# First weight by one casting load, phi transposed on chip, 128-row tiles of q, k and v, and 14 half tiles of output

## The chip, the cores and the metric

One NeuronCore of a Trainium2 chip. The metric is the device time of one execution in microseconds (us); lower is better. The profile's span runs from the first instruction of the program to the last.

## The reference

Two stages. First an attention over batch 4, 8 heads, 768 positions, head dimension 64, with scores `q k^T / 8`. Three of the heads (`is_retrieval`) use a causal mask. The other five keep, within the causal part, only the first 4 positions and a window of the last 64. A softmax over the keys and the product with `v` follow.

```python
scores = np.where(mask[None, :, :, :], scale * np.matmul(q, k.transpose(0, 1, 3, 2)), -1e9)
a = np.exp(scores - np.max(scores, axis=-1, keepdims=True))
a = a / (np.sum(a, axis=-1, keepdims=True) + 1e-09)
attn_out = np.matmul(a, v)
x = attn_out.transpose(0, 2, 1, 3).reshape(3072, 512)
```

Then a soft mixture of experts on the 3072 rows of `x`. `phi` is 512 x 32 (8 experts with 4 slots each), `w1` is 8 x 512 x 1024, `w2` is 8 x 1024 x 512, all float32.

```python
logits = x @ phi
d = softmax(logits, axis=0)              # over the 3072 rows
slot_input = (d.T @ x).reshape(8, 4, 512)
slot_out[e] = np.maximum(slot_input[e] @ w1[e], 0) @ w2[e]
out = softmax(logits, axis=1) @ slot_out.reshape(32, 512)
```

## The kernel before

**Order of the work.** The kernel does not write its instructions down directly. Each piece of work is an operation of a planner (`Plan`): a name, the engines that may run it with a cost for each, a due time (`key`), the operations it depends on, and the buffers it takes (`acq`) and gives back (`rel`). `Plan.run` places the operations one after another by these costs, and the instructions are emitted in that order. The list `SHIFTS` moves the due times of single operations and fixes some of them to ACT or DVE. Buffers come in classes: 11 large slots in SBUF (`S8`), two PSUM banks for transposes (`TR`), two for scores (`SC`), one for attention sums (`PV`), two memories each for transposed q and k (`QT`, `KT`), one for transposed v (`VT`), and so on. Within an engine the order is fixed by the plan.

**Loads.** All large loads go through POOL's DMA queue and cast float32 to bfloat16 on the way, in one order (`dma`, at most eight in flight). First come the halves of batch 0: q, k and v of heads pairs 0 and 1, then of 2 and 3, 768 KB of float32 each. Then w0, then q, k, v of batch 1, two weights, batch 2, three weights, batch 3, and the other weights. A weight has 2 MB of float32. w0 is special: its first quarter comes uncast, 512 KB over SP's queue, into the memory of `expT` (`sp_front`), and two POOL casts (`o_w0`) bring it into place; the other three quarters come by POOL's queue. SP's queue also brings the retrieval flags, once for each of 128 partitions, and phi by two loads whose contiguous pieces are 32 floats. The last five weights go into memory that attention gives back late; w14 and w15 (the last two of `w2`) come as halves of 256 output columns, first both left halves, then both right halves.

**Attention.** q, k and v arrive in rows of 32 positions. For batches 1 to 3 each of the nine (tensor, batch) loads fills 96 partitions of a slot. `transposes` turns it by four groups of 16 TensorE transposes (L577), each group evacuated by one copy of 768 elements per partition on DVE or ACT (L323, L321). There are 16 pairs `p = 4 b + n` of heads (n and n + 4). For a pair: five score products (`QK`, L610) of up to four 128 x 128 blocks for both heads, laid out by `PGROUPS`; an exponential on ACT for each (L679); three mask products on DVE (`MK`, L626), only for blocks on the diagonal and next to it; then `PV` (L740), its normalization (L761), and transposes of the result (`XT`, L773). One of the 21 blocks of a pair doesn't fit into the five groups: it is computed for all four pairs of a batch in a tile of its own (`QX`, exponential at L704). Before, that is block (0, 5): keys 0 to 127 for queries 640 to 767, which needs no mask.

**Experts.** At each batch's end `LG` (logits), `EL` (their exponential), `DS` (slot sums) and `TE`/`EE` (transposed exponentials into `expT`). After the last batch: `SI`, `H` (first layer, L915), `TH`, `W2` (second layer, L953, one step for each expert). In the gaps stand matmuls on zeros (`Z`, L902; `ZF`, L493, and `ZG`, L504, near the start).

**Output.** `RW` (L980) makes the sums of the row softmax by 24 small matmuls on PE, `RWR` (L986) their reciprocals on DVE; `SO` (L992, L994) puts half of the slot outputs into bfloat16. An output tile is one matmul (`OM`, L1009), a scaling by the reciprocal on ACT or DVE (`OE`, L1017, L1019), and a share of a store (`ST`, L1028). The first 12 of the 24 tiles of 128 rows are done in halves: the left 256 columns as soon as the left halves of w14 and w15 are there, stored over POOL's queue, and the right ones after the right halves, over SP's. The other 12 are done and stored whole, over SP's queue.

Of the kernel before, what the change touches and what calls it, by code (L numbers as in the profile page):

```python
# [10 lines left out]
F32 = mybir.dt.float32  # L11
# [5 lines left out]
KB = 512  # L17
# [144 lines left out]
def act(cols, extra=0.0):  # L162
# [4 lines left out]
SHIFTS = [-192, 84, -330, 309, -90, -87, 300, -18, 120, -42, -48, -360, -132, -240, 42, -360, 57, -222, 12,  # L167
# [28 lines left out]

PGROUPS = [
    [(0, 0, 4)],
    [(1, 1, 4)],
    [(2, 2, 4)],  # L200
    [(3, 3, 3), (0, 4, 1)],
    [(4, 4, 2), (5, 5, 1), (1, 5, 1)],
]
MGROUPS = [(0, 1), (2, 3), (4,)]
PCOL, PGRP = {}, {}
for _g, _parts in enumerate(PGROUPS):
    _c = 512 * _g
# [891 lines left out]
```

## Time and profile before

| | |
|---|---|
| median of the runs | 150.85 us (150.83, 150.85, 151.16) |
| the profiled execution | 150.66 us |
| its span | 148.9 us |
| PE, DVE, ACT, POOL busy | 84%, 73%, 73%, 23% of the span |
| read from HBM, written | 52.50 MB, 6.29 MB |
| mean granted TensorE clock | 0.959 |

The page divides the span into 40 slices of 3.7 us and gives for each the busy share of every engine, of the DMA engines, and the GB/s that they moved. The windows do the same for stretches that one chooses: for each, its length, the busy time and count of PE, PEld (weight loads), DVE, ACT and POOL, the granted clock, the DMA share and GB/s. A line of the timeline has the start, the time from there to the end of the last instruction that it merges, the engine, the line of the kernel, the operation with output and input, the count, and in brackets how long the engine had been idle and what ended that. A line of groups has busy time and mean nanoseconds of one instruction. A line of DMA issues has the count, the KB of each as written, and the us from issue to landing.

### The profile page before, as it was taken

The numbers are of one execution on the slowest core, as the hardware profiler recorded it, in microseconds if no ns is written. First come the engines' busy times: TensorE is split into PE (matmuls) and PEld (weight loads), VectorE is DVE, ScalarE is ACT, GpSimd is POOL, SyncE is SP. The second block draws the span as 40 slices with busy tenths as digits, with TensorE's granted clock in tenths as the row PEclk, the third lists the DMA queues.
The fourth block names the chain that finished last, engine by engine and source line by source line (L and its number), as shares of the span: only waits on it lengthen the run. The fifth ranks groups of instructions, "written<-read, shape, count | busy, mean of one in ns | idle before, by whom it ended". The sixth has DMA issues, their size and how long they took to land.

```text
span 148.9 us, 5316 instructions
## 1 busy us (share of the span) xinstructions
PE 124.9 (84%) x2351; PEld 85.2 (57%) x2351; DVE 109.0 (73%) x231; ACT 108.3 (73%) x139; POOL 34.2 (23%) x60
## 2 busy tenths in 40 slices
PE   6759999889999999998999999999959897659100
PEld 1256667568677676676766776756645553433000
DVE  1843699996999899999799999998974311749400
ACT  3134799989999978998799999999962450638300
POOL 6948411610201200310101104130170000520000
PEclk9999999999999999999999999999999999996855
DMA  5999999999999999999999999999999999999994
GB/s 116 162 209 211 227 205 216 216 214 216 210 217 215 216 216 212 212 218 214 215 214 214 216 214 217 216 212 215 216 215 212 203 198 198 166 328 308 390 425 207
DMA packets 14279, 33.18 MB, mean 223 GB/s; under 512 B 1392, under 2 KB 7024, under 8 KB 13872
## 3 DMA queue, kind: packets, MB, share of 16 engines
q0 software_dynamic: 11408, 27.53, 94.3%
q1 hardware_dynamic: 2848, 5.32, 10.0%
q8 instruction: 18, 0.29, 0.7%
q14 instruction: 5, 0.04, 0.1%
HBM read 52.50 MB, written 6.29 MB: 395 GB/s over the span
## 4 chain that ended last, share of the span: by engine, by line
PE 45%; DMA 20%; DVE 17%; ACT 7%; issue 4%; POOL 1%; DVEq 0%; ACTq 0%; POOLq 0%
DMA qk<-in_moe_w_dram 14%; PE pv L740 12%; PE sc L610 11%; PE tr L577 10%; ACT pt L679 6%; DMA slot<-in_q_dram 5%; DVE xv L761 4%; DVE pt L626 4%; PE bk L1009 3%; PE tr L773 3%; DVE vx L323 2%; PE tr L643 2%; DVE vf L658 2%; PE pv L504 2%; DVE slot L1019 1%
## 5 line engine op out<-in xcount | busy, mean ns | idle before, releaser
L679 ACT ACTIVATE pt<-sc 128x1024 bf16<-128x1024 f32 x80 | 76.8, 1042 | 6.0 <-PE sc L610 5.7
L610 PE MATMUL sc<-qk 64*128 64x128 bf16 (+3 forms) x288 | 32.5, 295 | 1.2 <-ACT pt L679 0.4
L626 DVE TENSOR_TENSOR pt<-pt,msk 128x1024 bf16<-128x1024 bf16 (+1 forms) x48 | 30.7, 658 | 2.1 <-ACT pt L679 1.8
L740 PEld LDWEIGHTS <-pt 128*128 128x128 bf16 x640 | 23.5, 97 | 8.6 <-issue 5.8
L740 PE MATMUL pv<-vx,pt 128*128 128x65 bf16 x352 | 26.3, 193 | 1.1 <-DVE xv L761 0.6
L577 PEld LDWEIGHTS <-slot 96*64 96x64 bf16 x768 | 20.4, 116 | 9.1 <-issue 5.8
L740 PE MATMUL pv<-vf,pt 128*128 128x65 bf16 x288 | 21.6, 194 | 1.0 <-DVE xv L761 0.9
L577 PE MATMUL tr<-ident,slot 96*64 96x96 bf16 x576 | 17.1, 208 | 0.5 <-DVE qk L323 0.5
L610 PEld LDWEIGHTS <-qk 64*128 64x128 bf16 x288 | 11.9, 94 | 8.6 <-issue 2.4
L323 DVE COPY qk<-tr 128x768 bf16<-128x768 bf16 x23 | 12.3, 551 | 6.2 <-PE tr L577 6.2
L761 DVE TENSOR_TENSOR xv<-pv,rs 128x768 bf16<-128x768 f32 (+1 forms) x17 | 15.5, 910 | 0.6
L334 POOL DMA_DIRECT2D slot<-in_moe_w_dram x11 | 7.6, 695 | 31.8 <-PE tr L577 26.7
L321 ACT COPY qk<-tr 128x768 bf16<-128x768 bf16 x9 | 7.2, 810 | 5.8 <-PE tr L577 5.7
L1017 ACT ACTIVATE slot<-bk,rrow 128x256 f32<-128x256 f32 (+1 forms) x17 | 8.1, 553 | 4.2 <-PE bk L1009 4.2
L1019 DVE TENSOR_SCALAR slot<-bk,rrow 128x256 f32<-128x256 f32 (+1 forms) x19 | 9.3, 560 | 0.6 <-PE bk L1009 0.5
L773 PE MATMUL tr<-ident,xv 128*128 128x128 bf16 x96 | 8.4, 220 | 1.3 <-issue 0.5
L577 PE MATMUL tr<-ident_u,slot 96*64 96x96 bf16 x192 | 7.7, 245 | 1.5 <-DMA slot<-in_q_dram 1.5
L323 DVE COPY xv<-tr 128x768 bf16<-128x768 bf16 x15 | 8.0, 552 | 0.8 <-PE tr L577 0.8
L1009 PE MATMUL bk<-msk,expT 128*128 128x256 bf16 (+1 forms) x36 | 7.8, 365 | 0.9 <-DVE msk L994 0.7
L323 DVE COPY vx<-tr 128x768 bf16<-128x768 bf16 x15 | 8.2, 549 | 0.0
L323 DVE COPY xT<-tr 128x768 bf16<-128x768 bf16 (+1 forms) x14 | 7.3, 524 | 1.1 <-PE tr L773 1.0
L643 PE MATMUL tr<-ident,xv 128*128 128x128 bf16 x96 | 8.1, 220 | 0.0
(102 smaller groups left out, 146.8 us busy)
## 6 DMA issues: line engine op xcount, KB each, us to landing
slot<-in_moe_w_dram POOLq DMA_DIRECT2D x10, 1024.0 KB, 25.2
out_dram<-slot SPq DMA_DIRECT2D x3, 1024.0 KB, 6.8
slot<-in_q_dram POOLq DMA_DIRECT2D x3, 768.0 KB, 30.2
slot<-in_k_dram POOLq DMA_DIRECT2D x3, 768.0 KB, 32.0
slot<-in_v_dram POOLq DMA_DIRECT2D x3, 768.0 KB, 22.7
out_dram<-slot SPq DMA_DIRECT2D x3, 512.0 KB, 3.8
qk<-in_moe_w_dram POOLq DMA_DIRECT2D x1, 1024.0 KB, 19.2
vx<-in_moe_w_dram POOLq DMA_DIRECT2D x1, 1024.0 KB, 22.2
```

Source lines behind the costliest of these rows:

```text
L323: nc.vector.tensor_copy(dst, src)
L577: nc.tensor.transpose(dst_, rv[:, i, 8 * c + s, :], idv)
L610: nc.tensor.matmul(scb[sc.slot][:, i, c:c + 128 * nb], kk, qq.rearrange("p b c -> p (b c)"), start=True, stop=True)
L626: nc.vector.tensor_tensor(pT, pT, mh, op=ALU.mult)
L643: nc.tensor.transpose(t[:, 128 * j:128 * (j + 1)], vT[:, 6 * n + j, :], ident)
L679: nc.scalar.activation(pTs[PTb[b, n].slot][:, :, 512 * g:512 * (g + 1)], scb[sc.slot], ACT.Exp, scale=scale)
L740: nc.tensor.matmul(pvb[:, h, 65 * i:65 * (i + 1)], lt, rhs, start=(j == 0), stop=(j == i))
L761: nc.vector.tensor_tensor(xo, pvw[:, :, :, 0:64], r.rearrange("p i (j o) -> p i j o", o=1).to_broadcast([P, 2, i1 - i0, 64]), op=ALU.mult)
L773: nc.tensor.transpose(t[:, 128 * i:128 * (i + 1)], xv[:, i, 128 * n:128 * (n + 1)], ident)
L1009: nc.tensor.matmul(banks[bf.slot][:, 0:w], out_lhs(gi, r), slot_out[:, cs], start=True, stop=True)
L1017: nc.scalar.activation(d, banks[bf.slot][:, 0:w], ACT.Copy, scale=sc_)
L1019: nc.vector.tensor_scalar(d, banks[bf.slot][:, 0:w], sc_, None, op0=ALU.mult)
```

## The change

Six things.

- **w0** comes like the other weights: one load of 2 MB on POOL's queue. The load on SP's queue and POOL's two casts are gone, and so is the waiting for them.
- **phi** is loaded by one DMA of 128 rows of 4 x 32 floats, cast, transposed by four matmuls, copied with its columns rearranged, transposed back by four, and copied.
- **The flags** are loaded once, into one partition; a matmul with a row of ones spreads them over the partitions.
- **Tiles of 128 rows**: q, k and v of batches 1 to 3 are packed into seven tiles, six of 128 rows and one of 96, of parts of one or two tensors (13 loads instead of nine). A tile is transposed in four groups of 16, and each part of a group is evacuated by a copy of its own. The order of loads interleaves them with the weights.
- **Scores**: block (5, 5) takes the place of (0, 5) in the shared tile. It lies on the diagonal, so it gets its mask there (`MX`, a DVE product for each exponential of that tile), and the third mask product of a pair has 256 columns for each head instead of 384.
- **Output**: 14 instead of 12 tiles in halves; the first right-hand store covers two tiles instead of four; `RW` no longer waits for `W2` of expert 0 and is due 10 us earlier in the plan. Fewer and longer matmuls on zeros near the end, and half of the `ZG` ones.

All of `SHIFTS` is replaced.

```diff
 PGROUPS = [
     [(0, 0, 4)],
     [(1, 1, 4)],
     [(2, 2, 4)],
-    [(3, 3, 3), (0, 4, 1)],
-    [(4, 4, 2), (5, 5, 1), (1, 5, 1)],
+    [(3, 3, 3), (1, 5, 1)],
+    [(4, 4, 2), (0, 4, 2)],
 ]
+TILES = [
+    [("q", 1, 0, 24), ("k", 1, 0, 8)],
+    [("k", 1, 8, 24), ("v", 1, 0, 16)],
+    [("v", 1, 16, 24), ("q", 2, 0, 24)],
+    [("k", 2, 0, 24), ("v", 2, 0, 8)],
+    [("v", 2, 8, 24), ("q", 3, 0, 16)],
+    [("q", 3, 16, 24), ("k", 3, 0, 24)],
+    [("v", 3, 0, 24)],
+]
+TKEYS = [10.8, 16.0, 31.0, 36.0, 50.0, 60.5, 68.4]
...
     def sp_front(o):
-        nc.sync.dma_start(w0f, moe_w1[0].rearrange("(di x) f -> di (x f)", x=4)[:, 0:2 * KB])
         nc.sync.dma_start(ri, ri_src)
-        pv_ = moe_phi.rearrange("(i n d) s -> i d n s", i=2, n=4)
-        for i in range(2):
-            nc.sync.dma_start(phf[64 * i:64 * (i + 1)], pv_[i])
+        nc.sync.dma_start(phf, moe_phi.rearrange("(p a) s -> p (a s)", a=4))
...
-    for x in range(8):
+    for x in range(4):
         o_z = pl.op(f"ZG{x}", pe(52, 4), 105.0, deps=[o_z], lead=7.8 + 0.7 * x, emit=emit_zg, mode="full", mm=4)
...
+    o_fp = pl.op("flag product", on("PE", 0.07, 0.27), -10, deps=[o_fr, o_tab], acq=[flb], mode="r32", mm=1,
+                 emit=lambda o: nc.tensor.matmul(trb[flb.slot][:, 0:H], unit[:, 0:128], frow, start=True, stop=True))
...
+    o_p = pl.op("phi cast", on("DVE", 0.2), T * 2.0, deps=[o_sp], lead=7.0, emit=lambda o: nc.vector.tensor_copy(phw, phf))
+    o_p = pl.op("phi T1", pe(56, 4), T * 2.1, deps=[o_p, o_id], acq=[pb1], emit=phi_t1, mode="c32", mm=4)
+    o_p = pl.op("phi E1", copy_engs(512), T * 2.2, deps=[o_p], rel=[pb1], emit=phi_e1)
+    o_p = pl.op("phi T2", pe(40, 4), T * 2.3, deps=[o_p], acq=[pb2], emit=phi_t2, mode="r32", mm=4)
...
     load_w(0)
-    o_w0 = [pl.op(f"w0 cast {x}", on("POOL", 1.2), 27.0, deps=[o_sp, wland[0]], lead=26.5 + 1.5 * x,
-                  emit=lambda o, x=x: nc.gpsimd.tensor_copy(
-                      slots[wbuf[0].slot][:, KB * x:KB * (x + 1)], w0f[:, KB * x:KB * (x + 1)])) for x in range(2)]
-    batch_loads(1)
+    load_tile(0)
+    load_tile(1)
     load_w(1)
+    load_tile(2)
     load_w(2)
-    batch_loads(2)
+    load_tile(3)
+    load_tile(4)
     for i in (3, 4, 5):
         load_w(i)
-    batch_loads(3)
+    load_tile(5)
+    load_tile(6)
...
+    def tile_transposes(ti):
+        parts = TILES[ti]
+        R = 4 * sum(x1 - x0 for _, _, x0, x1 in parts)
+        tbs = [({"q": QTb, "k": KTb, "v": VTb}[x][b], x0 == 0) for x, b, x0, _ in parts]
+        for c in range(4):
...
+            a = pl.op(f"T.{ti}.{c}", pe(29.5 if R == 128 else 23, 16), key, deps=tland[ti] + [o_id] + [tb.op for tb, _ in tbs],
+                      acq=[tr] + [tb for tb, new in tbs if new and c == 0], rel=[tbuf[ti]], emit=emit_t, mode="c64",
+                      mm=16)
...
-                pT, mh = pT[:, :, 2048:2432], mh[:, :, 256:640]
+                pT, mh = pT[:, :, 2048:2304], mh[:, :, 256:512]
...
+            e = pl.op(f"MX.{b}.{ns[0]}", on("DVE", 0.07 + 0.134 * len(ns)), key + 0.3, deps=[e] + [o_hm[n] for n in ns],
+                      emit=emit_mx)
...
-    a = pl.op("RW", on("PE", 0.7, 0.27), kt + 24, deps=[eto[b] for b in range(B)] + [o_st, w2o[0]], acq=[rw], emit=emit_rw,
+    a = pl.op("RW", on("PE", 0.7, 0.27), kt + 14, deps=[eto[b] for b in range(B)] + [o_st], acq=[rw], emit=emit_rw,
               mode="full", mm=24)
...
-    NL = 3
+    NL = 14
+    halved = [(gi, min(4, NL - 4 * gi)) for gi in range((NL + 3) // 4)]
...
+        for r0, r1 in [(0, 2), (2, 4)] if gi == 0 else [(0, n)]:
+            store("SP", "r", gi, r0, r1, slice(256, 512), kt + 41 + gi + 0.1 * r0)
```

More of the change, by code (lines that the diff above doesn't have):

```diff
@@ L262 @@
     ident_r = sb.tile([P, P], BF16, name="ident_r")
-    phf = sb.tile([P, 4, NS], F32, name="phf")
+    phf = sb.tile([P, 4 * NS], F32, name="phf")
     phi = sb.tile([P, 4, NS], BF16, name="phi")
@@ L336, in dma @@
         took = nbytes / 425000.0
-        chain.append(pl.op("land " + name, {"DMA": (took, took + 1.3 + min(2.1, 0.22 * len(chain)))}, -100, deps=[iss] + chain[-1:], lead=3.4))
+        chain.append(pl.op("land " + name, {"DMA": (took, took + 1.3 + min(2.1, 0.22 * len(chain)))}, -100, deps=[iss] + chain[-1:], lead=3.2))
         return chain[-1]
@@ L517, with phi_t1 @@
     o_st = pl.op("slot tables", on("DVE", 1.3), -70, deps=[o_id], emit=slot_tables)
-    o_phi = pl.op("phi", on("DVE", 0.15), T * 1.5, deps=[o_sp], lead=15.0, emit=lambda o: nc.vector.tensor_copy(phi, phf))
-    def batch_loads(b):
-        for x in "qkv":
-            load_part(x, b)
+    pb1, pb2 = Buf("TR"), Buf("TR")
+    phw = phi.rearrange("p n s -> p (n s)")
+    def phi_t1(o):
+        t = tr_bf(pb1.slot, DM)[0:NS]
+        for a in range(4):
+            nc.tensor.transpose(t[:, P * a:P * (a + 1)], phw[:, NS * a:NS * (a + 1)], ident)
@@ new lines, in phi_e1, with phi_t2 @@
+    def phi_e1(o):
+        copy(o, t1.rearrange("s (n i y a) -> s n i y a", n=4, i=2, a=4),
+             tr_bf(pb1.slot, DM)[0:NS].rearrange("s (a i n y) -> s n i y a", a=4, i=2, n=4))
+    def phi_t2(o):
+        for n in range(4):
+            nc.tensor.transpose(tr_bf(pb2.slot, 4 * NS)[:, NS * n:NS * (n + 1)], t1[:, 128 * n:128 * (n + 1)],
+                                ident[0:NS, 0:NS])
+    o_p = pl.op("phi cast", on("DVE", 0.2), T * 2.0, deps=[o_sp], lead=7.0, emit=lambda o: nc.vector.tensor_copy(phw, phf))
@@ L549, in dst_of, with transposes @@
         return {"q": lambda: qTs[QTb[b].slot], "k": lambda: kTs[KTb[b].slot], "v": lambda: vT}[x]
-    def transposes(x, b):
-        raw = raws[x, b]
-        tb = {"q": QTb, "k": KTb, "v": VTb}[x][b]
-        dst = dst_of(x, b)
-        first = True
-        for part in ((0, 1) if b == 0 else (None,)):
+    def transposes(x):
+        raw, tb, dst, first = raws[x, 0], {"q": QTb, "k": KTb, "v": VTb}[x][0], dst_of(x, 0), True
+        for part in (0, 1):
             es = []
-            for c in range(2 if b == 0 else 4):
+            for c in range(2):
@@ L593, in transposes @@
-                es.append(pl.op(f"E{x}{b}.{part or 0}.{c}", copy_engs(768), key, deps=[a], rel=[tr], emit=emit_e))
-                first = False
-            if b == 0:
-                ev[x, 0, part] = es
-            else:
-                ev[x, b] = es
+                            nc.tensor.transpose(t[64 * i:64 * (i + 1), :, :, s, :], rv[:, i, 8 * c + s, :], ident_u)
+                a = pl.op(f"T{x}0.{part}.{c}", pe(23, 16), key, deps=[lands[x, 0, part], o_iu, tb.op],
+                          acq=[tr] + ([tb] if first else []), rel=[raw], emit=emit_t, mode="c64", mm=16)
@@ L600, in evs @@
     def evs(x, b, n):
-        return ev[x, 0, n // 2] if b == 0 else ev[x, b]
+        return ev[x, 0, n // 2] if b == 0 else [e for x0, x1, e in ev[x, b] if x0 < 6 * n + 6 and x1 > 6 * n]
     def sc_mms(sc, b, parts):
@@ L624, in f @@
             else:
-                pT, mh = pT[:, :, 2048:2432], mh[:, :, 256:640]
+                pT, mh = pT[:, :, 2048:2304], mh[:, :, 256:512]
             nc.vector.tensor_tensor(pT, pT, mh, op=ALU.mult)
         return f
-    for b in range(B):
-        for x in "qkv":
-            transposes(x, b)
+    for x in "qkv":
+        transposes(x)
+    for ti in range(len(TILES)):
+        tile_transposes(ti)
     for b in range(B):
```

140 lines of the change are left out of this document (75 added, 65 removed), and 57 rows, old and new, of the table SHIFTS.

## The prediction

> **What bounds the kernel now.** I read the page first (busy shares, the 40 slices, the queues), then the windows by stage, the table of DMA issues, and the timeline at both ends. The page:
>
> ```profile
> PE 124.9 (84%) x2351; PEld 85.2 (57%) x2351; DVE 109.0 (73%) x231; ACT 108.3 (73%) x139; POOL 34.2 (23%) x60
> DMA  5999999999999999999999999999999999999994
> GB/s 116 162 209 211 227 205 216 216 214 216 210 217 215 216 216 212 212 218 214 215 214 214 216 214 217 216 212 215 216 215 212 203 198 198 166 328 308 390 425 207
> HBM read 52.50 MB, written 6.29 MB: 395 GB/s over the span
> ```
>
> No engine fills the span, but the DMA row is full from the second slice to the last. GB/s counts bytes as written: a casting load reads four bytes for each two that it writes, so 214 there is about 428 GB/s of HBM reads. All inputs (52.5 MB) are read once, and all output (6.29 MB) written once. The windows say where the transfers fall short:
>
> ```profile
> 0.00:2.00 2.00, 0.85 (x3) 0.41 (x4) 0.24 (x1) 1.27 (x1) 0.88 (x5) 1.00 0.06 14
> 2.00:5.00 3.00, 2.04 (x7) 0.45 (x5) 1.36 (x4) 0.60 (x3) 2.92 (x9) 1.00 0.99 185
> 5.00:9.00 4.00, 2.49 (x7) 0.73 (x6) 3.68 (x18) 0.00 (x0) 3.53 (x8) 1.00 1.10 194
> 9.00:15.00 6.00, 5.97 (x88) 4.55 (x88) 1.54 (x5) 2.92 (x5) 3.90 (x8) 1.00 1.15 211
> 20.00:108.00 88.00, 84.33 (x1818) 61.60 (x1815) 81.40 (x159) 83.94 (x98) 15.01 (x21) 1.00 1.06 214
> 119.00:127.00 8.00, 7.14 (x138) 3.96 (x131) 1.39 (x3) 2.54 (x4) 0.00 (x0) 1.00 1.45 197
> 129.00:131.00 2.00, 0.36 (x9) 0.17 (x9) 0.88 (x3) 0.69 (x2) 1.99 (x3) 1.00 0.90 242
> 131.00:134.00 3.00, 2.08 (x20) 1.41 (x20) 1.77 (x5) 1.25 (x4) 0.17 (x1) 0.89 0.95 322
> 134.00:135.00 1.00, 1.00 (x5) 0.40 (x3) 1.00 (x3) 0.99 (x3) 0.00 (x0) 0.50 0.66 225
> 135.00:139.00 4.00, 3.12 (x11) 1.02 (x9) 4.00 (x8) 3.47 (x6) 0.00 (x0) 0.78 1.00 340
> 139.00:147.00 8.00, 0.00 (x0) 0.00 (x0) 0.56 (x1) 0.14 (x1) 0.00 (x0) 0.57 1.02 420
> ```
>
> The last two columns are DMA share and GB/s. From 20 to 108 us the load stream runs at a flat 214 with no hole, so compute time saved there moves nothing by itself. What can move the end is the first 9 us (14, 185, 194), the hand-over to the stores (129 to 135) and the stores of half rows (340 where whole rows get 420). But compute isn't far behind: in the same 88 us PE is busy 84.3, ACT 83.9 and DVE 81.4. At the hand-over the two nearly meet:
>
> ```profile
> 124.62 0.39 PE L953 MATMUL bk<-pt,xT 128*32 128x256 bf16 x8
> 125.87 0.40 PE L953 MATMUL bk<-qk,xT 128*32 128x256 bf16 x8 [0.86 <-DMA qk<-in_moe_w_dram]
> 126.20 0.66 PEld L980 LDWEIGHTS <-expT 128*128 128x128 bf16 x24 [0.21 <-issue]
> 126.32 0.47 ACT L992 ACTIVATE msk<-bk,rcs 128x256 bf16<-128x256 f32 x1 [4.13 <-PE bk L953]
> 126.80 0.80 PEld L1009 LDWEIGHTS <-expT 128*128 128x128 bf16 x8
> 126.99 0.31 DVE L986 RECIPROCAL rrow<-bk 128x24 f32<-128x24 f32 x1 [3.31 <-PE bk L980]
> 127.39 2.30 ACT L1017 ACTIVATE slot<-bk,rrow 128x256 f32<-128x256 f32 x6 [0.59 <-PE bk L1009]
> 128.22 2.96 POOL L1028 DMA_DIRECT2D out_dram<-slot  x4 [17.50 <-DVE slot L1019]
> 133.74 6.36 SPq L1028 DMA_DIRECT2D out_dram<-slot  x6
> ```
>
> PE waited 0.86 us for w15's first half at 125.87; that is all the slack compute has there. The start:
>
> ```profile
> 0.73 0.37 SPq L461 DMA_DIRECT2D expT<-in_moe_w_dram  x1
> 1.33 0.79 POOL L334 DMA_DIRECT2D slot<-in_q_dram  x1 [0.89 <-POOLq L1080]
> 5.07 2.42 PE L493 MATMUL sc<-zt 128*128 128x448 bf16 x6
> 9.03 1.49 PE L577 MATMUL tr<-ident_u,slot 96*64 96x96 bf16 x32 [1.54 <-DMA slot<-in_q_dram]
> 11.37 0.85 PE L577 MATMUL tr<-ident_u,slot 96*64 96x96 bf16 x16
> 15.01 1.94 ACT L679 ACTIVATE pt<-sc 128x1024 bf16<-128x1024 f32 x2 [1.95 <-PE sc L610]
> expT<-in_moe_w_dram SPq DMA_DIRECT2D x1, 512.0 KB, 4.5
> phf<-in_moe_phi_dram SPq DMA_DIRECT2D x2, 32.0 KB, 9.1
> out_dram<-slot POOLq DMA_DIRECT2D x1, 128.0 KB, 3.3
> ```
>
> The first load of q, issued at 1.33, is used only at 9.03.
>
> **Part 1, the front of the DMA stream.** Written by 9 us: 14x2 + 185x3 + 194x4 KB = 1.36 MB. Off this come w0's float quarter on SP (0.524 MB), 0.008 MB of flags and some 0.06 MB of phi; the casting stream wrote 0.77 MB, 3.6 us at 214 GB/s: a stream that starts at 5.4 us. By 5 us it had written 0.05 MB, a start at 4.8; the other 0.6 us went between 5 and 9, where phi comes in 512 rows of 128 bytes.
>
> The change takes all this out of its way: no quarter, one packet of flags, phi in 128 rows of 512 bytes ahead of q. But the quarter must now go through the casting stream: 0.262 MB more written, 1.22 us at 214. When would the stream start? Early bound: SP's issue at 0.73 had moved 28 KB by 2.0, at the 185 of the next row 0.15 us, so 1.1 us from issue to data; 1.33 + 1.1 = 2.4. Late bound: only phi's 0.6 us comes back, 4.8. Nearest row: POOL's own 128 KB store, 3.3 us to landing, 3.0 without its 0.3 us of data at 420; half of that ahead of the data gives 2.8, and I add 0.5 for the slow first rows (185, not 214, even from 2 to 5): 3.3 us. Gain 5.4 - 3.3 - 1.22 = 0.9 us; bounds -0.6 (later) and +1.8.
>
> The Trainium skill, "DMA: Bandwidth & Descriptors", "Specifications", speaks against the move: it gives about 0.6 us to the first byte of a transfer issued by SP, about 1 us for one issued by POOL, and calls the SP path generally faster. SP's 1.1 us here is longer than its 0.6. By its 1 us, an estimate, POOL's stream would start at 2.3 and the gain would be 1.9 us; the lost head start on SP is already in the sum.
>
> **Part 2, compute at the front and middle.** q's first half at 1.33 + 3.0 + 393 KB/214 = 6.2 us lies ahead of the second run of zero matmuls, which ends at 7.5; transposes start then, not at 9.03: 1.5 us sooner. k follows about 1.9 us behind q, so by 9, not 11.37: 2.4 sooner. With half of the small fillers (L504) gone, the first exponential comes 1.5 to 3 us before 15.01. The flags gain a matmul and wait for PE behind those zeros; queued behind them on DVE are the first masks. Masks are first used after the first exponentials, so a us of delay is covered; uncovered it would cost that us at the start of compute, not of the DMA.
>
> The added DVE work:
>
> ```profile
> L626 DVE TENSOR_TENSOR pt<-pt,msk 128x1024 bf16<-128x1024 bf16 x32 | 22.0, 699 | 1.1 <-ACT pt L679 0.8
> L626 DVE TENSOR_TENSOR pt<-pt,msk 128x768 bf16<-128x768 bf16 x16 | 9.1, 576 | 1.0 <-ACT pt L679 1.0
> L323 DVE COPY qk<-tr 128x768 bf16<-128x768 bf16 x23 | 12.3, 551 | 6.2 <-PE tr L577 6.2
> L323 DVE COPY xT<-tr 128x384 bf16<-128x384 bf16 x2 | 0.7, 352 | 0.4 <-PE tr L773 0.4
> ```
>
> Masks: 123 ns for 256 elements, so 512 take 453. The 16 third masks shrink from 768 to 512 (-2.0 us); the diagonal block moved to the shared tile needs 2x453 + 3x699 (+3.0): +1.0. Evacuations for batches 1 to 3: 36 copies become 52 of the same total; 551 and 352 give a fixed 153 ns a copy, 16 more cost 2.4 us, shared between DVE and ACT. Phi's second cast, two copies and eight small transposes: some 0.8 us. PE: 36 groups of 96 columns against 24 of 128 and 4 of 96: equal columns; two 128-column score matmuls become one of 256: nothing. Together some 4 us on DVE and ACT, which have 6.6 and 4.1 us idle of 88. I take 1.5 us of it on the path, between none and 3.4 (masks and copies). Compute then ends about a us sooner.
>
> Moved waits: a tile that holds the tail of k and the head of v can be transposed only when the previous batch's v buffer is free. k2 waits so for the last V2 of batch 1, with the scores of pair 8 behind it; the planner can pull that forward, since both vb buffers are there. POOL's queue gets four more issues, but its loads run far ahead, as the unbroken 214 shows. The two casts that leave POOL (w0) hid in its 23% share: nothing.
>
> **Part 3, the hand-over.** The first output scaling (127.39) waited for the reciprocal (126.99 to 127.30), which waited for the 24 sums behind W2 of w15. With the sums earlier, it waits for SO.0 (126.79) and a matmul of some 0.3: about 127.1, 0.25 us sooner. The 24 weight loads (0.66 us) move in front of W2's last step, onto slack: 0.86 + 1 from part 2 - 0.9 (w15 lands sooner) - 0.66 = 0.3. Without that cover they'd cost their 0.66 on the path.
>
> **Part 4, the stores.** At 134 to 135 the share is 0.66: left stores are done, right ones not begun: 0.34 us lost. Two more left tiles (0.26 MB, 0.8 us at 322) and a first right store of two tiles (one round of scaling less, about 0.5 us) close it. Two more tiles written in halves: 0.524 MB at 340, not 420: 0.29 us. Sum: 0.05 gained (bounds -0.3, +0.4).
>
> The Trainium skill, same page and section, asks 512 bytes and more for line rate; halves have rows of 1,024 bytes. By it the two tiles would cost nothing and part 4 would gain 0.34. The row of 340 beside 420 disagrees with it, and I go by the rows.
>
> **Sum.** The profiled execution took 150.66 us (span 148.9 and 1.8 around it); the runs' median is 150.85. 150.66 - 0.9 - 0.25 - 0.05 = 149.46; plus 0.19 for the median: 149.65, say 149.7.
>
> **Rivals.**
> - *DVE becomes the bound.* Copies and masks all lie on the path (3.4 us), k2's wait among them, against 1.5 us sooner at the start, and the sums' 0.66: compute at the hand-over 2.6 later, less the slack of 0.86 it is 1.7 later, and the stores with it, less 0.25: about 152.3. It decides once compute there comes more than 0.9 us later than now. For it: 81 to 84 busy of 88. Against: the first exponential should come up to 3 us sooner. 0.17.
> - *The head start was real.* POOL's stream starts at 4.8 with or without the quarter: 0.6 lost, 0.3 from parts 3 and 4: 151.15. For it: nothing shows POOL's first transfer alone. Against: the store's 3.3 us. 0.15.
> - *The stream starts as soon as SP's did* (2.4), and compute keeps ahead: 150.85 - 1.8 - 0.25 - 0.3 = 148.5. The page's 1 us leads to the same. 0.12.
>
> **Numbers.** Forecast 0.56. About 0.3% (0.45 us) is what a measurement of this kernel can tell from no change. Faster: 0.52 of the forecast, 0.12 and 0.03 of the second rival, 0.67. Same: 0.14. Slower: 0.02 of the second rival and the first's 0.17, 0.19. The range reaches from just under the third rival, 148.3, to 151.6, past the second; above it is most of the first. The forecast's own range is 148.8 to 150.5.
>
> **What would show it.** Right: transposes of q from about 7.5 us, the first exponential near 12 to 13.5; 5 to 9 us above 205 GB/s; w15's first half used near 125 us with PE waiting for it; reciprocal of the sums well before; no window of 0.66 between left and right stores. Wrong: GB/s near zero until 4 us or more; a hole in the 214 between 20 and 108; or W2's last step released by DVE, ACT or PE and not by DMA.

## The result, and the profile after

The changed kernel took 150.22 us (median of 8 runs, 149.78 to 150.46), the kernel before 151.03 us beside it (150.69 to 151.97): 0.9932 of its time, interval [0.9904, 0.9959]. Figures leave out executions more than 1.5% above the fastest of their kernel: five of the twelve of e11_oldfront (152.41 to 154.49 us), two of the 23 of the kernel before beside it, none elsewhere. The ratios are worked out from the single executions, not from the medians. By its ratio the change is worth 1.0 us, by the medians 0.8. The profiled execution took 150.36 us, with a span of 148.6. The page of after; slices of 3.7 us:

```profile
span 148.6 us, 4999 instructions
PE 126.1 (85%) x2179; PEld 83.4 (56%) x2179; DVE 111.2 (75%) x253; ACT 107.1 (72%) x143; POOL 35.6 (24%) x63
DMA  2999999999999999999999999999999999999994
GB/s 30 195 211 213 216 212 213 212 221 210 214 215 217 214 212 213 215 217 213 213 214 215 212 217 219 210 215 213 215 213 218 205 196 196 162 331 343 378 429 181
HBM read 52.49 MB, written 6.29 MB: 396 GB/s over the span
```

The first slice fell from 116 to 30 GB/s: only the flags and phi (0.07 MB) go over SP's queue ahead of the casting loads now. From the third slice on the stream is as flat as it was. The dip to 162 where loads give way to stores is still there. The windows:

```profile
0.00:2.00 2.00, 0.84 (x3) 0.40 (x4) 0.24 (x1) 1.26 (x1) 0.88 (x5) 1.00 0.00 0
2.00:5.00 3.00, 2.12 (x8) 0.47 (x6) 1.05 (x5) 0.61 (x3) 2.92 (x9) 1.00 0.76 108
5.00:9.00 4.00, 4.00 (x42) 2.26 (x42) 2.93 (x14) 0.12 (x1) 4.00 (x9) 1.00 1.12 209
9.00:15.00 6.00, 6.00 (x87) 4.09 (x84) 3.96 (x11) 3.34 (x5) 4.24 (x11) 1.00 1.13 213
20.00:108.00 88.00, 84.87 (x1662) 60.37 (x1661) 80.97 (x175) 82.89 (x103) 15.38 (x22) 1.00 1.06 214
129.00:131.00 2.00, 1.08 (x18) 0.34 (x16) 1.84 (x6) 0.78 (x3) 1.98 (x3) 1.00 0.86 247
131.00:134.00 3.00, 2.56 (x17) 1.61 (x18) 2.62 (x8) 2.26 (x7) 0.79 (x2) 1.00 0.98 344
134.00:135.00 1.00, 1.00 (x6) 0.43 (x5) 1.00 (x4) 1.00 (x3) 0.00 (x0) 1.00 1.02 347
135.00:139.00 4.00, 0.94 (x4) 0.20 (x2) 3.15 (x5) 1.93 (x4) 0.00 (x0) 1.00 1.04 358
139.00:147.00 8.00, 0.00 (x0) 0.00 (x0) 0.00 (x0) 0.00 (x0) 0.00 (x0) 0.62 0.96 384
```

By 9 us 108x3 + 209x4 KB = 1.16 MB were written; less 0.07 for phi that is 1.09 MB of casting loads, 5.1 us at 214: the stream starts at 3.9 us, not at the 3.3 of the forecast. The share at 134 to 135, 0.66 before, is 1.02: that hole is closed. From 20 to 108 DVE is busy 80.97 us (81.40 before) and ACT 82.89 (83.94). Now the timeline of after, at its start and at the hand-over:

```profile
1.32 0.80 POOL L345 DMA_DIRECT2D slot<-in_q_dram  x1 [0.88 <-POOLq L1136]
7.34 1.49 PE L604 MATMUL tr<-ident_u,slot 96*64 96x96 bf16 x32
11.61 0.18 PE L518 MATMUL tr<-xT 1*128 1x8 bf16 x1
12.89 1.02 ACT L725 ACTIVATE pt<-sc 128x1024 bf16<-128x1024 f32 x1
...
117.63 0.74 PE L1034 MATMUL bk<-cols,expT 128*128 128x1 bf16 x24
118.40 0.31 DVE L1040 RECIPROCAL rrow<-bk 128x24 f32<-128x24 f32 x1 [0.57 <-PE bk L1034]
126.10 0.39 PE L1007 MATMUL bk<-qk,xT 128*32 128x256 bf16 x8
127.38 1.27 DVE L1073 TENSOR_SCALAR slot<-bk,rrow 128x256 f32<-128x256 f32 x3 [2.43 <-PE bk L1063]
128.16 3.64 POOL L1082 DMA_DIRECT2D out_dram<-slot  x5 [16.31 <-DVE slot L1073]
130.24 0.40 PE L1007 MATMUL bk<-qk,xT 128*32 128x256 bf16 x8 [0.55 <-DMA qk<-in_moe_w_dram]
132.24 5.53 SPq L1082 DMA_DIRECT2D out_dram<-slot  x5
```

Compute starts as forecast: transposes of q at 7.34, the first exponential at 12.89 instead of 15.01. But at 126.10 PE goes through the left half of w15 without a wait: compute got there no sooner than the data. And the first left store is issued at 128.16, before at 128.22.

To see where time goes behind 120 us, the execution can be added up from the trace's DMA records: what the loads still had to move at 120 us, at their 214 GB/s; the stores at their own rates (345 GB/s for half rows, as in the windows with a share near 1 from 131 to 135; 420 for whole ones); and what is left over, time in which the engines moved less than that. Times taken from the records rather than from a view, here and below (first and last data, first and last exponentials), count from 0.05 us before the zero of the views. Everything in us:

| profiled execution | time | loads left at 120 | stores | lost | last data |
|---|---|---|---|---|---|
| before | 150.66 | 8.27 | 16.61 | 2.43 | 147.31 |
| before, another execution (e13_before) | 151.51 | 8.44 | 16.61 | 3.10 | 148.15 |
| before with the new tail (e12_before_tail) | 150.49 | 8.29 | 16.88 | 2.06 | 147.22 |
| after with the old front (e14_front_cast) | 150.89 | 8.53 | 16.88 | 2.25 | 147.66 |
| after | 150.36 | 7.98 | 16.88 | 2.15 | 147.02 |

The load stream of after is 0.29 us ahead (8.27 to 7.98) and its stores have 0.27 more to do. The rest of the gain lies in the column of lost time, and there the two executions of before differ by 0.67 us; the one that the prediction was made from, 150.66 us, lies 0.4 under the median of before. The experiments have to say what makes that column.

### The profile page after: what moved, and what is told of

It reads as the page before. It is cut to its first block, busy times and chain, and to the rows that moved or that the text cites. A ratio compares the mean times of both kernels' runs of the same rounds, so it can differ in the third digit from the quotient of the medians.

```text
span 148.6 us, 4999 instructions
## 1 busy us (share of the span) xinstructions
PE 126.1 (85%) x2179; PEld 83.4 (56%) x2179; DVE 111.2 (75%) x253; ACT 107.1 (72%) x143; POOL 35.6 (24%) x63
## 4 chain that ended last, share of the span: by engine, by line
PE 33%; DVE 29%; DMA 13%; ACT 9%; issue 4%; POOL 3%; DVEq 0%; POOLq 0%; ACTq 0%
DMA qk<-in_moe_w_dram 13%; PE pv L794 8%; PE sc L655 8%; DVE pt L671 7%; ACT pt L725 7%; PE tr L604 5%; DVE xv L815 5%; DVE vx L334 3%; PE tr L630 3%; DVE qk L334 3%; DVE slot L1073 3%; DVE vf L704 2%; DVE xv L334 2%; PE tr L689 2%; DVE xT L334 2%
## 5 line engine op out<-in xcount | busy, mean ns | idle before, releaser
L655 PE MATMUL sc<-qk 64*128 64x512 bf16 (+3 forms) x256 | 33.6, 323 | 2.5 <-ACT pt L725 2.0
L671 DVE TENSOR_TENSOR pt<-pt,msk 128x1024 bf16<-128x1024 bf16 (+1 forms) x48 | 28.3, 595 | 2.7 <-ACT pt L725 2.2
L630 PE MATMUL tr<-ident,slot 128*64 128x128 bf16 (+1 forms) x448 | 16.7, 219 | 0.9 <-ACT qk L332 0.6
L655 PEld LDWEIGHTS <-qk 64*128 64x128 bf16 x256 | 10.5, 95 | 10.3 <-issue 3.6
L630 PEld LDWEIGHTS <-slot 128*64 128x64 bf16 (+1 forms) x448 | 13.2, 109 | 5.3 <-issue 5.0
L334 DVE COPY qk<-tr 128x768 bf16<-128x768 bf16 (+2 forms) x29 | 13.4, 485 | 3.0 <-PE tr L604 2.6
L332 ACT COPY qk<-tr 128x768 bf16<-128x768 bf16 (+2 forms) x11 | 6.7, 610 | 5.4 <-PE tr L604 4.4
L334 DVE COPY xv<-tr 128x768 bf16<-128x768 bf16 (+2 forms) x20 | 8.3, 430 | 1.3 <-PE tr L604 0.9
L604 PEld LDWEIGHTS <-slot 96*64 96x64 bf16 x192 | 7.4, 156 | 3.4 <-issue 3.1
L604 PE MATMUL tr<-ident_u,slot 96*64 96x96 bf16 x192 | 8.9, 269 | 0.0
```

What stands on the lines that cost most here:

```text
L334: nc.vector.tensor_copy(dst, src)
L604: nc.tensor.transpose(t[64 * i:64 * (i + 1), :, :, s, :], rv[:, i, 8 * c + s, :], ident_u)
L630: nc.tensor.transpose(t[64 * i:64 * (i + 1), :, s, :], rv[:, i, 8 * c + s, :], ident[0:R, 0:R])
L655: nc.tensor.matmul(scb[sc.slot][:, i, c:c + 128 * nb], kk, qq.rearrange("p b c -> p (b c)"), start=True, stop=True)
L671: nc.vector.tensor_tensor(pT, pT, mh, op=ALU.mult)
```

## The experiments

Each of the single edits has the changed kernel's order of work written out and fixed, so that the planner does not move anything else; e0_after is the changed kernel in that form, and e2_twelve and e9_sixteen are planned anew, which leaves the order the same up to the output. e12_before_tail and e13_before start from the kernel before.

**e0_after.** No edit but the fixed order.

> The changed kernel with its order of operations, engines and buffers written out as a list instead of planned (the frozen order that the next experiments edit). Both theories: as the changed kernel, 150.2 us, some 0.99 of before.

Measured 150.06 us, 0.9932 [0.9906, 0.9957]. Its profile ran another course at the start. The transposes of batch 0 are the same instructions in every execution, so their busy time tells the pace of TensorE. Windows of their line alone (PE, weight loads, granted clock, DMA share, GB/s) in e0_after, then in after, then in e2_twelve:

```profile
16.00:20.00 4.00, 2.08 (x42) 1.71 (x44) 0.50 1.06 214
```

```profile
12.00:16.00 4.00, 2.32 (x48) 1.97 (x48) 1.00 1.13 216
20.00:26.00 6.00, 1.71 (x32) 1.33 (x32) 1.00 1.07 214
```

```profile
12.00:16.00 4.00, 1.40 (x48) 1.24 (x48) 1.00 1.13 216
20.00:26.00 6.00, 1.06 (x32) 0.83 (x32) 1.00 1.07 216
```

At the granted clock of 0.50 a transpose took 50 ns in e0_after. In after it took 48 and 53 ns, in e2_twelve 29 and 33. So after ran at half pace there too, though its rows say 1.00: its trace has no record of the clock before 24.9 us, and the views (and the mean clocks of the pages) count a stretch without a record as 1.00. In every profile the first matmuls run ahead of the first record and at the slow pace. Counting that time, and later stretches at 0.50, as half pace, the five profiles with the same front and the same masks line up:

| profile | half pace before 26 us | third pair's first exponential | last exponential |
|---|---|---|---|
| e2_twelve | 10.5 | 24.20 | 105.45 |
| e9_sixteen | 14.2 | 24.83 | 106.11 |
| e4_sums_gaps | 15.6 | 25.97 | 107.19 |
| e0_after | 18.4 | 27.19 | 108.32 |
| after | 24.9 | 28.45 | 109.67 |

The difference exists by the third and fourth pair of heads; from there the executions run in step. The profiles of before and e12_before_tail follow the same rule: half pace until 17.3, 16.6 and 15.0 us, last exponential at 108.55, 108.05 and 107.80. Yet the five executions took 150.17 to 150.56 us, and not in that order: compute's finish moves by 4 us without moving the end.

**e1_quarter.** w0's first quarter comes over SP's queue again, with the casts on POOL, behind the flags' one packet.

```diff
         nc.sync.dma_start(ri, ri_src)
+        nc.sync.dma_start(w0f, moe_w1[0].rearrange("(di x) f -> di (x f)", x=4)[:, 0:2 * KB])
...
```

> Undoes one part: w0's first quarter comes uncast over SP's queue again, with POOL's two casts; phi and flags stay new, the order of all else is frozen. Theory A (the end follows the load stream): the casting stream starts at about 4.8 instead of 3.9 us but writes 0.26 MB (1.2 us) less, so it ends 0.3 us sooner: 149.9. Theory B (compute arrives last at the hand-over, the stream's end is not what counts): q lands later, which compute loses again before pair 4; no change, 150.2, W2's last left step released by PE or DVE.

Measured 149.91 us, 0.9913 [0.9887, 0.9938]: the same as with the quarter moved. At 120 us its loads had 7.99 us left, against 7.98. The casting stream starts 1.2 us later (counted back at 214 GB/s from the bytes moved by 9 us: 5.1 against 3.9) and has 1.22 us less to move. Its hand-over shows something else; timeline and windows of e1_quarter:

```profile
125.07 0.40 PE L1098 MATMUL bk<-qk,xT 128*32 128x256 bf16 x8 [0.40 <-DMA qk<-in_moe_w_dram]
127.19 3.64 POOL L1173 DMA_DIRECT2D out_dram<-slot  x5 [18.22 <-DVE slot L1164]
131.81 0.40 PE L1098 MATMUL bk<-qk,xT 128*32 128x256 bf16 x8 [3.08 <-DMA qk<-in_moe_w_dram]
133.92 3.60 SPq L1173 DMA_DIRECT2D out_dram<-slot  x5
```

```profile
134.00:135.00 1.00, 1.00 (x7) 0.70 (x5) 1.00 (x4) 0.83 (x3) 0.00 (x0) 0.50 0.35 127
```

The first left store goes out 0.97 us sooner than in after (127.19), but the right half of w15 is used 1.57 us later (131.81). The last packets of that load start at 131.09 us, in after at 129.73; the likely reason is that they share the engines with stores that began sooner. The first right store comes at 133.92, its first data at 134.90, and in between the share is 0.35. What the earlier hand-over gains is given back in a hole a few us later. In after the left stores start later and run until 135.66; the right half is used sooner (130.24), the first right store is queued at 132.24, well ahead of their end, and there is no hole.

**e2_twelve.** 12 half tiles again, and the first right store of four tiles; the early sums stay.

```diff
-    NL = 14
+    NL = 12
...
-        for r0, r1 in [(0, 2), (2, 4)] if gi == 0 else [(0, n)]:
+        for r0, r1 in [(0, n)]:
```

> Undoes the stores: 12 half tiles and a first right store of four tiles. The prediction's sum: the hole of 0.34 us between left and right stores comes back, 0.29 us of slower half rows goes: 150.2 to 150.3. Rival: half rows cost nothing while other traffic is there, then the hole alone counts: 150.5 to 150.6.

Measured 149.48 us (149.25 to 150.70, two groups), 0.9909 [0.9876, 0.9942]. The profiled execution is of the upper group, 150.56 us, and shows the hole at its widest:

```profile
131.00:134.00 3.00, 1.94 (x15) 1.08 (x15) 1.37 (x4) 0.67 (x2) 0.00 (x0) 0.50 0.74 281
134.00:135.00 1.00, 1.00 (x6) 0.69 (x5) 1.00 (x4) 0.83 (x3) 0.00 (x0) 0.50 0.03 12
```

From 133 to 136 us the share is 0.22, with PE busy all the time at a granted clock of 0.50: 2.3 us lost there. Stores that ran faster between 128 and 133 us make up for much of it; the lost time as a whole is 3.05 us, 0.9 more than in after. But five of the seven executions took 149.25 to 149.51 us, less than any of the 14 of after and e0_after (149.59 at the least). The ratios, 0.9909 and 0.9932, do not tell 12 tiles from 14; they do say that 14 tiles are not what made the kernel faster. Neither expectation came true: both had this kernel at 150.2 or more.

**e4_sums_gaps.** The 24 sums in three parts of eight, each put where PE waits between the first and second layer.

```diff
+    for x in range(3):
+        def emit_rw(o, x=x):
+            for gi in (2 * x, 2 * x + 1):
...
```

> The 24 sums of the row softmax are split into three groups of eight and put into waits of PE in the expert layers (before TH.0, before the first W2 step, before the W2 step that waits for HE.1), instead of all ahead of the first layer. Theory A: no change, 150.2 (within 0.1). Theory B: the first layer starts 0.7 us sooner, W2's last left step comes 0.5 to 0.7 sooner, and the end 0.4 to 0.6: 149.7.

Measured 150.36 us, 0.9949 [0.9927, 0.9970]. Early or in the gaps, the sums cost nothing that shows. The first left store went out at 126.87 us, 1.3 sooner than in after, and it was given back as in e1_quarter: the share at 134 to 135 was 0.10.

**e6_nomasks.** The third mask product of each pair and the shared tile's (`MX`) are left out, 21 products on DVE; their masks aren't applied.

```diff
-                                    emit=mask_emit(b, n, m))
+                                    emit=mask_emit(b, n, m) if m < 2 else None)
...
-                      emit=emit_mx)
+                      emit=None)
```

> The frozen changed kernel without its third mask product of each pair and without the masks of the shared tile (21 DVE products left out, some 10 us of DVE time; that part of the output is unmasked). Theory of the prediction's first rival (DVE, or compute in the middle, bounds the end): the last exponential 1 to 4 us sooner and the end with it, 149 or less. Theory A (from 20 us on the end follows the load stream and the hand-over): within 0.3% of 150.06, whenever the last exponential comes.

Measured 150.12 us, 0.9939 [0.9915, 0.9963], as the changed kernel. The time of these products on DVE does not set the end.

**e8_oldphi.** phi in pieces of 128 bytes again, without the turning on chip.

```diff
-        nc.sync.dma_start(phf, moe_phi.rearrange("(p a) s -> p (a s)", a=4))
+        pv_ = moe_phi.rearrange("(i n d) s -> i d n s", i=2, n=4)
+        for i in range(2):
+            nc.sync.dma_start(phf[64 * i:64 * (i + 1)].rearrange("p (n s) -> p n s", n=4), pv_[i])
...
```

> The frozen changed kernel with phi loaded as before, by two DMAs in pieces of 32 floats, and without the two transposes and two copies on chip. Theory A with part 1's bookkeeping: the stream loses about 0.6 us between 3 and 11 us, w15's halves land 0.6 later and the end is 0.4 to 0.6 later: 150.5 to 150.7. Rival (small packets only fill holes of the engines): GB/s of 5 to 9 us as in the changed kernel, no change, 150.06.

Measured 150.13 us, 0.9946 [0.9925, 0.9967]. Counted back from the bytes moved by 20 us, its casting stream starts at 4.2 us; the six profiles with the new loading of phi and w0 have 3.9 to 4.05. At 120 us the loads had 8.25 us left, against 7.9 to 8.1 in those six: the short pieces cost about 0.25 us of the stream, though the median doesn't show it. The Trainium skill ("DMA: Bandwidth & Descriptors", "Specifications") puts the least size for full rate at 512 bytes; phi's pieces of 128 and 512 bytes lie on either side of that, and the 0.25 us agree with it.

**e9_sixteen and e10_combo.** 16 half tiles; and 16 half tiles with the quarter on SP's queue and the sums in the gaps.

```diff
-    NL = 14
+    NL = 16
```

> 16 half tiles instead of 14, all else as changed. Theory C (the hole between left and right stores comes and goes with how early the left ones start, and 14 tiles are too few when they start before 129): no hole in the profile; 0.2 to 0.5 sooner than 14 where the hand-over is early, 0.1 to 0.2 later (two more tiles of slow half rows) where it is late: 149.7 to 150.2. Theory of part 4's sum alone: 0.3 later than 14, 150.35.

> Three edits together: w0's quarter on SP's queue, the 24 sums in PE's waits, 16 half tiles. Theory A and C: the stream ends 0.3 sooner, left stores start near 128.9, and 16 tiles fill the hole: 149.4 to 149.7. If the early hand-over is given back even so: 149.9 to 150.1.

Measured 150.17 us, 0.9941 [0.9921, 0.9961], and 149.96 us, 0.9926 [0.9904, 0.9948]. Lost time falls to 1.55 and 1.54 us, and the stores have 0.27 us more to do; the medians do not tell them from the changed kernel.

None of these edits alone takes the gain away. So the parts were taken together: the front as a whole, and the tail as a whole.

**e11_oldfront.** The changed kernel with the front as before: the quarter of w0 first on SP's queue and cast on POOL, the flags in 128 partitions, phi in short pieces.

```diff
     def sp_front(o):
+        nc.sync.dma_start(w0f, moe_w1[0].rearrange("(di x) f -> di (x f)", x=4)[:, 0:2 * KB])
         nc.sync.dma_start(ri, ri_src)
-        nc.sync.dma_start(phf, moe_phi.rearrange("(p a) s -> p (a s)", a=4))
+        pv_ = moe_phi.rearrange("(i n d) s -> i d n s", i=2, n=4)
+        for i in range(2):
+            nc.sync.dma_start(phf[64 * i:64 * (i + 1)].rearrange("p (n s) -> p n s", n=4), pv_[i])
...
```

> The changed kernel, its order of work frozen, with the whole front as before: a quarter of w0 in float on SP's queue ahead of everything and cast on POOL, the flags as one row in each of 128 partitions, phi in two transfers of 128-byte pieces and no turning on chip. The tiles of 128 rows, the 14 half tiles and the early sums stay. Front theory (the 0.9 us come from the first microseconds): the time goes back to that of the kernel before, 150.7 to 151.0. Tail theory (they come from the stores of half tiles and the early sums): 150.1 as the changed kernel, between 149.8 and 150.4, although the stream of casting loads starts near 5.4 us again. Half and half: 150.5. If neither holds and only the middle (the tiles of 128 rows) matters, it is 150.1 too, and the next run tells these apart.

Measured 150.99 us (150.06 to 152.28): 1.000 [0.996, 1.004]. Beside it the kernel before spread too, from 150.15 to 152.32 (median 151.13). Neither theory had foreseen such a spread. The profile is of the execution of 150.06 us; its timeline and its DMA issues say what stood at the front:

```profile
11.96 0.23 DVE L634 CAST phi<-phf 128x128 bf16<-128x128 f32 x1 [4.54 <-DMA phf<-in_moe_phi_dram]
```

```profile
expT<-in_moe_w_dram SPq DMA_DIRECT2D x1, 512.0 KB, 4.6
phf<-in_moe_phi_dram SPq DMA_DIRECT2D x2, 32.0 KB, 8.9
```

phi landed 8.9 us after its issue, behind the 512 KB of w0. In the changed order its cast is the first thing on DVE ahead of the copies of q (at 7.34 in after, where phi lands in 1.8 us), so DVE stood for 4.54 us and the first exponential came at 15.97. Yet this execution is as short as those of the changed kernel: the late start by itself cost it nothing.

**e12_before_tail.** The kernel before with the tail alone changed: 14 half tiles, a first right store of two tiles, the early sums. The matmuls on zeros stay as they were.

```diff
-    NL = 3
...
+    NL = 14
+    halved = [(gi, min(4, NL - 4 * gi)) for gi in range((NL + 3) // 4)]
...
-    a = pl.op("RW", on("PE", 0.7, 0.27), kt + 24, deps=[eto[b] for b in range(B)] + [o_st, w2o[0]], acq=[rw], emit=emit_rw,
+    a = pl.op("RW", on("PE", 0.7, 0.27), kt + 14, deps=[eto[b] for b in range(B)] + [o_st], acq=[rw], emit=emit_rw,
...
```

> The kernel before with the tail of the change alone: 14 half tiles in place of 12, the first right store of two tiles, the sums for the slot weights ahead of the last products; front, middle and their order are those of the kernel before up to the sums. Front theory: 151.0, as before (150.8 to 151.1). Tail theory: 150.1, with no window of less than 0.9 between the left and the right stores. Half and half: 150.5. If the gain lies in the middle it stays at 151.0 while the run with the old front stays at 150.1.

Measured 150.41 us, from 150.15 to 150.81 in 12 runs: 0.9950 [0.9922, 0.9979]. The tail by itself brings some 0.75 us [0.32, 1.18], on the old front and the old middle, and here the spread is small.

```profile
120.66 0.74 PE L980 MATMUL bk<-cols,expT 128*128 128x1 bf16 x24
125.97 0.40 PE L953 MATMUL bk<-qk,xT 128*32 128x256 bf16 x8
128.09 1.43 POOL L1028 DMA_DIRECT2D out_dram<-slot  x2 [18.13 <-DVE slot L1019]
```

From the last left step of the second layer to the first left store it is 2.12 us now, where it was 128.22 - 125.87 = 2.35.

**e13_before.** The kernel before, unchanged, for a second profile.

> The kernel before, unchanged, for a second profile of it. Its first profile is of an execution that took 150.66 us, under its median of 151.0. If executions differ only in how far compute gets before the hand-over, the last exponential will start at another time than 108.55 us, by a us or more, with the data ending within 0.5 us of 147.31. If the executions of this kernel differ at the hand-over instead, the share of the transfers between 134 and 136 us is under 0.66 in a slower one, and the end is later by the time lost there, 0.3 to 0.5 us.

Its execution took 151.51 us. Timeline and windows:

```profile
126.57 0.40 PE L953 MATMUL bk<-qk,xT 128*32 128x256 bf16 x8 [2.06 <-DMA qk<-in_moe_w_dram]
127.69 0.31 DVE L986 RECIPROCAL rrow<-bk 128x24 f32<-128x24 f32 x1 [4.51 <-PE bk L980]
128.92 2.96 POOL L1028 DMA_DIRECT2D out_dram<-slot  x4 [18.70 <-DVE slot L1019]
```

```profile
129.00:131.00 2.00, 1.03 (x12) 0.41 (x11) 1.58 (x5) 1.38 (x4) 1.90 (x3) 1.00 0.65 139
134.00:135.00 1.00, 1.00 (x7) 0.70 (x5) 1.00 (x3) 0.83 (x3) 0.00 (x0) 0.50 1.00 348
135.00:139.00 4.00, 3.54 (x16) 1.52 (x14) 3.93 (x8) 3.85 (x8) 0.00 (x0) 0.87 0.85 291
```

The last exponential began at 108.05 us, only 0.5 from the first profile's 108.55: compute isn't the difference, and of the two things expected it is the second, at other places: the share is 1.00 at 134 to 135 and 0.40 at 135 to 136. The left half of w15 landed 0.7 us later (126.57 against 125.87), though the loads as a whole were 0.17 us behind. PE stood for 2.06 us, long enough for all 24 sums, which then ran behind it. The transfers ran short twice: the share is 0.65 at 129 to 131, until the late left store, and 0.85 at 135 to 139, with the first right data at 135.95 and the last left data at 135.71. Less the 0.34 us that it does not lose at 134 to 135, that is about the 0.67 us more of lost time.

**e14_front_cast.** e11_oldfront with the cast of phi behind the first masks, the only change.

```diff
-phi cast|DVE|;Tq0.0.0|PE|1,0;issue q1.0|POOL|4;
+Tq0.0.0|PE|1,0;issue q1.0|POOL|4;
...
-MK.0.1|DVE|;EX.1.1|ACT|;phi T1|PE|0;
+MK.0.1|DVE|;phi cast|DVE|;EX.1.1|ACT|;phi T1|PE|0;
```

> The run with the whole front as before once more, with one thing changed: the cast of phi on DVE stands behind the first masks instead of ahead of DVE's first copy. In that run phi landed 8.9 us after its issue, behind the quarter of w0, DVE waited 4.54 us for it at 11.96 and the first exponential came at 15.97 us; its times spread from 150.06 to 154.49. Cover theory (that start took compute's cover, and the old front's transfers themselves cost no more than 0.3 us): the first exponential comes at 13 to 14 us, the spread falls to under 1 us and the time to 150.1 to 150.5. Front theory (the old front costs by its transfers, whatever waits for phi): 150.9 to 151.5, with the spread of that run or near it. Chance of 150.5 to 150.9: a front worth about half of the gain.

Measured 150.71 us (150.05 to 151.44), 0.9957 [0.9928, 0.9985]; the first exponential at 14.22. By the ratios, one cast in another place took 0.65 us off (1.000 to 0.9957), but the two intervals overlap a little: likely, not shown. What is left of the difference to after is the old front's: some 0.4 us by the ratios (0.9957 against 0.9932, whose intervals overlap), the middle case of the three expected. Timeline and windows:

```profile
126.24 0.40 PE L1099 MATMUL bk<-qk,xT 128*32 128x256 bf16 x8 [1.74 <-DMA qk<-in_moe_w_dram]
128.36 3.64 POOL L1174 DMA_DIRECT2D out_dram<-slot  x5 [18.29 <-DVE slot L1165]
```

```profile
129.00:131.00 2.00, 0.88 (x11) 0.31 (x10) 1.81 (x5) 0.93 (x3) 1.95 (x3) 1.00 0.90 221
134.00:135.00 1.00, 1.00 (x7) 0.69 (x6) 1.00 (x3) 0.83 (x3) 0.00 (x0) 0.50 1.01 348
135.00:139.00 4.00, 3.11 (x14) 1.33 (x12) 3.92 (x8) 3.87 (x8) 0.00 (x0) 0.87 1.04 361
```

This is the counterpart of e13_before: loads just as late (8.53 us left at 120), PE waiting 1.74 us for w15, but the new tail. The share at 129 to 131 is 0.90 in place of 0.65, at 135 to 139 it is 1.04 in place of 0.85, and the lost time is 2.25 us in place of 3.10.

## Why the prediction was right, and where its sum was not

The forecast, 149.7 us, is 0.5 under the 150.22 measured; sign and range hold. The change is worth 0.8 us between the medians, or 1.0 by the ratio, where the sum had 1.2. That the total came so near is in part luck: the front was given 0.6 us too much and the tail, parts 3 and 4, some 0.4 too little.

**Part 1, the front of the stream: 0.9 forecast, 0.3 measured.** The step that failed is the start of the stream. The forecast took half of a store's landing time for POOL's latency and came to 3.3 us. The windows of after:

```profile
2.00:3.00 1.00, 1.00 (x5) 0.33 (x3) 0.00 (x0) 0.02 (x1) 0.93 (x3) 1.00 0.59 82
3.00:4.00 1.00, 0.58 (x2) 0.00 (x0) 0.63 (x1) 0.09 (x1) 1.00 (x4) 1.00 0.68 55
4.00:5.00 1.00, 0.55 (x3) 0.14 (x3) 0.42 (x4) 0.50 (x2) 1.00 (x4) 1.00 1.02 186
```

Of the 82 KB between 2 and 3 us some 66 are phi and flags; the casting rows come at 55 GB/s from 3 to 4 us and near full rate only then, 2.7 us after the issue at 1.32. By the 1 us to the first byte that the Trainium skill gives for POOL ("DMA: Bandwidth & Descriptors", "Specifications") the stream would have started at 2.3, an estimate; the trace doesn't agree, its first packet of a casting load starts at 2.82 us. That moving the quarter is worth nothing, e1_quarter shows (7.99 us left either way); e8_oldphi puts some 0.25 us of the 0.3 on phi, where the forecast had read 0.6 for phi alone. The rival that the head start was real had it right that moving the quarter brings nothing, but not that it costs 0.6: the stream did start 1.2 us sooner, just the time that the quarter takes in it.

**Part 2, compute: the start right, the rest not.** Transposes at 7.5 were forecast and came at 7.34, the first exponential between 12 and 13.5 came at 12.89. "Compute ends about a us sooner" is wrong for the profile of after: the last exponential began at 109.67, 1.1 us later than before, and PE had no wait left at 126.10. Over the five profiles with this front it holds: 107.3 on average, against 108.1 in the three with the old front and middle. What the forecast left out is the pace of TensorE in the first 25 us. It ran at half pace until 24.9 us in after and until 17.3 in the profile that the forecast was made from; so the head start of 2.1 us was gone by the third pair of heads, whose first exponential came at 28.45 (26.57 before). The added work itself was sized about right: copies on DVE and ACT, phi's two among them, take 54.0 us in all against 51.3, masks 31.9 against 31.6, where the forecast had 3.2 and 1.0 more.

Nor does an early finish pay. In six of the nine profiles from after to e10_combo W2's last left step came at 124.77 to 125.23 us with PE waiting for w15, as forecast, and the first left store up to 1.4 us sooner than before (126.83 to 127.29), but they took 149.91 to 150.56 us, as the others. So the rival that DVE becomes the bound falls: its point was passed by 0.2 us in the profile of after (126.10 without a wait, against 125.87 with one), and e6_nomasks gets nothing for 21 products fewer. Whether the long executions of e11_oldfront are those in which compute came late was not seen in a profile.

**Part 3, the sums: 0.25 forecast, 0.23 to 0.29 measured** from W2's last left step to the store: 2.35 us in both profiles of before, 2.12 in e12_before_tail and e14_front_cast, 2.06 in after. The sums rode on slack, as forecast, wherever PE waited for w15. In after itself there was no slack (the forecast had 0.3), and the store left as late as before, 128.16 against 128.22.

**Part 4, the stores: 0.05 forecast; by themselves they gain nothing that shows.** The whole tail is worth 0.75 us [0.32, 1.18] in e12_before_tail, 0.65 [0.23, 1.09] with the middle in e14_front_cast; less the 0.25 of part 3 some 0.4 to 0.5 are left. But e2_twelve, which takes part 4 back, is no slower (0.9909 against 0.9932). Two more half tiles cost 0.27 us at the stores' rates (0.52 MB at 345 instead of 420), where 0.29 was forecast. The step that failed is the hole: 0.34 us were read from one profile, and closing it was priced as if it were always there. Whether there is one goes with the time from the first left store to the first use of w15's right half. With 14 tiles the share at 134 to 135 is 0.94 or more where that time is 2.1 to 3.3 us (after, e0_after, e8_oldphi and the three with parts of before), and 0.35, 0.10 and 0.12 where it is 4.6 to 4.8 (e1_quarter, e4_sums_gaps, e6_nomasks). With 12 tiles there is a hole at 3.0 us already (before, and e13_before a us later) and the widest, 2.3 us, at 4.6 (e2_twelve); with 16 the share is 0.91 and 1.00 at 4.6 to 4.7. So more left tiles do cover a longer wait, as forecast, but no median shows a gain by it. The granted clock does not decide it: it is 0.50 there in e14_front_cast, without a hole, as in e1_quarter.

What stays open: which part of the tail carries the gain. e2_twelve, with 12 tiles, has all of it; so the early sums are the likelier part, although they would then be worth more than the 0.25 us that they save ahead of the first store. The changed kernel with its sums late again was not run. The tiles of 128 rows, the moved score block and the new zeros were not run by themselves either; e14_front_cast has them and e12_before_tail does not, and with 0.9957 and 0.9950 they bring nothing that shows. What decides when TensorE gets its full clock at the start is not known: it differs between executions of one order of work.

## What to carry to other kernels

Where the DMA engines are busy from end to end, moving bytes from one queue to another moves nothing: a start that comes 1.2 us sooner was paid with 1.22 us of bytes; better-shaped packets gained a little (phi, 0.25 us). The time is then made where loads give way to stores: keep the chain from the last load to the first store short, put work that waits for nothing into the engine's wait ahead of it, and do not count on an earlier first store alone, for here it was given back in a hole before the second group of stores. Read a small hole from more than one execution before pricing it: 0.34 us in one profile was 0 to 2.3 us in others. And check the pace of an engine by the same instructions in two profiles: here a clock shown as 1.00 was only a clock without a record.

## What the runs showed of the hardware

- A store on SP's queue waits longer for its first data while POOL's stores are queued: issued at 132.24 us in after, it moved its first data 2.48 us later, when the left stores were nearly done; in e1_quarter, where the share had fallen to 0.35, it took 0.93 us from the issue at 133.92.
- A first casting load issued by POOL at 1.32 us moved 55 GB/s between 3 and 4 us and 186 between 4 and 5.
- TensorE ran its first matmuls at half pace in every profile (48 to 53 ns for a transpose that takes 29 to 33 later). Its clock's first record, 1.00, came between 8.0 us (e6_nomasks) and 24.9 us (after) with the new order, and in e0_after, e4_sums_gaps, e6_nomasks and e8_oldphi it fell back to 0.50 from some 15 us to 22 to 25. Between 10.5 and 24.9 us at half pace the last exponential moved from 105.45 to 109.67 us, with no effect on the time that shows.
